# Prologue of a fused attention + MoE kernel: S by the second queue, k features from PSUM on three engines, a shorter token scale, smaller weight loads

## Chip, cores, metric

One core of a Trainium2 chip. The metric is the device time of one execution in microseconds (us), median of several runs. A kernel with one core has no second die to compare with, so a run's "state" is read from its time alone: **slow** is a run over 1.5% above the fastest run of the same kernel, all others are fast. In the profile PE is TensorE, PEld its weight loads, DVE VectorE, ACT ScalarE, POOL GpSimd, SP SyncE; a "q" behind a name is that engine's queue of DMA issues. L309 is line 309 of the kernel that the profile is of, so the same operation has another line in another kernel.

## The reference

```python
# q, k, v: (4 batches, 4 heads, 1088 tokens, 32); S1, S2: (8, 32); w_in (128, 2048), w_out (2048, 128)
def phi(x):                                  # 64 features: all products of two 8-wide projections
    a = einsum('rd,bhsd->bhsr', S1, x);  b = einsum('rd,bhsd->bhsr', S2, x)
    return einsum('bhsi,bhsj->bhsij', a, b).reshape(..., 64)
q_p, k_p = phi(q), phi(k)
kv = einsum('bhsf,bhsd->bhfd', k_p, v);  z = sum(k_p, axis=2)
x = einsum('bhsf,bhfd->bhsd', q_p, kv) / (einsum('bhsf,bhf->bhs', q_p, z) + 1e-6)
x = x.transpose(0, 2, 1, 3).reshape(4352, 128)
h = maximum(x @ w_in, 0);  out = (h * h) @ w_out        # all in fp32 at the boundary
```

## The kernel before

The loop over blocks of 384 tokens (FFN1, relu, square, FFN2, and the attention of later batches between them) is bound by TensorE and is all but untouched. What the change touches is the **prologue**: everything between the start and the first FFN2 matmul (tile `po`). Names to keep in mind: `s_T` is S1 and S2 transposed; `sk` and `sr` are spread copies of it; `kT` is k transposed; `kf` the projections of k, `kp` the 64 features of k; `kvp` collects the kv and z sums over nine tiles of 128 tokens; `rep` are the projections of q, each replicated over the rows that need it; `qp` the features of q; `nd` numerator and denominator; `xs` the scaled tokens that FFN1 takes. `keep_warm` issues fp16 matmuls of zeros with 512 columns, put there to bring TensorE to full clock.

```python
    WARM0, WARM = 9, 4
    ...
    nc.scalar.dma_start(s_nat[0:8, :], S1[:, :])          # ACT's queue
    load_qk(kn[0], k, 0, 0, 512)                          # SP's queue from here on
    nc.sync.dma_start(s_nat[8:16, :], S2[:, :])
    load_qk(kn[0], k, 0, 512, S)
    ...
    a_kT(0, 0)                                            # DVE transposes: kT first,
    nc.vector.transpose(s_T[:, :], s_nat[:, :])           # then S
    ...
    keep_warm(WARM0)
    a_kf(0, 0, psf, "pg");  a_fs(0, 0)                    # two tiles of k, ACT copies them out
    keep_warm(1, x0)
    a_kf(0, 1, psf, "pg");  a_fs(0, 1)
    ...                                                   # tiles 4 to 8 of k by another form
    replicated(2, ...)
    a_kp(0, 0);  a_kp(0, 1)                               # DVE: features of tiles 0 to 3
    ...                                                   # DVE: one transpose, features of tiles 4 to 8
    replicated(0, x0[:, 0:512])
    for t in range(4):  a_kv(0, t);  a_z(0, *st[0, "kp", t], False)
    ...
    for t in range(4, 9):  a_kv(0, t);  a_z(0, *st[0, "kp", t], t == 8)
    nc.scalar.copy(qb[:, :], rep[2][:, 0:384])
    products(0)                                           # DVE: features of q, first half
    replicated(1, x0[:, 512:1024])                        # into the tile that products(0) read
    a_kvz(0);  products(1);  a_set(2);  a_qT(0, 384, 768);  a_qT(0, 768, S)
    a_kvs(0);  a_nd(0, 0);  a_kvT(0);  a_kw(0)
    a_qc(0, 1, psf, "po")                                 # q projections of the next block
    keep_warm(WARM)
    a_x1(0, 0);  a_x2(0, 0)                               # token scale
    a_x3(...);  a_xp(...);  a_xT(...)                     # xs, transposed for FFN1
```

## Time and profile before

| | us |
|---|---|
| kernel before, runs beside the changed kernel | 193.72 median of 4 (193.23 to 194.33) |
| kernel before, all 50 runs of the study | 192.3 to 197.0 |
| span in its profile (the time less some 1.8 of launch) | 193.1 |

The profile that the prediction quotes was taken while TensorE ran at a quarter of its clock. In the prediction that quarter is my estimate; `b0_before` bears it out: the first warm-ups follow each other at 0.84 us in the quoted profile and at 0.43 in `b0_before`, and those at 14.56 us in `b0_before` at 0.21, a quarter of 0.84. So the first experiment, `b0_before`, runs the unchanged kernel once more and gives a profile at full clock; all readings of "before" below are from it. Its timeline, in columns start, duration, engine, line, operation, out<-in with the shapes, count, and in brackets how long the engine idled and what ended that:

```profile
1.00 3.75 PE L1055 MATMUL warm<-zero 128*128 128x512 f16 x9 [1.00 <-DVE s_nat L167]
...
4.90 0.63 PE L329 MATMUL kf<-sk,kT 128*128 128x64 f32 x4 [0.15 <-ACT sk L302]
...
7.24 1.53 PE L1083 MATMUL rep<-qT,sr 128*128 128x384 f32 x4
...
10.24 0.54 DVE L1088 TENSOR_TENSOR qp<-rep,qb 128x384 f32<-128x384 f32 x1
...
11.16 0.32 DVE L444 STREAM_TRANSPOSE kvt<-kvp 128x128 f32<-128x128 f32 x1 [0.38 <-PE kvp L405]
...
17.67 0.49 PE L931 MATMUL po<-g,w_o 128*128 128x128 f32 x2
```

The chain is: warm-ups up to `kf` at 4.90 with a gap of 0.15, the replications of q, the first product of q at 10.24 (early: `kvp` is still being summed), `kvt` at 11.16, the first FFN2 at **17.67**.

### The profile page before, as it was taken

What the parts mean: (1) busy time and instruction counts of PE and PEld (TensorE: products, weight loads), DVE (VectorE), ACT (ScalarE), POOL (GpSimd) and SP (SyncE); (2) the same over time, 40 slices, a digit from 0 to 9 for tenths busy, and PEclk for the clock granted to TensorE, in tenths of its full rate; (3) what the DMA queues carried; (4) which work ended last, traced back from release to release, by engine and by line L of the source; (5) the groups of instructions that cost most, each with busy time, mean ns of one, the idle gap of its engine ahead of it and who ended that gap; (6) DMA issues with size and microseconds to landing.
All of it is one profiled execution on the core that took longest, in us unless ns stands there. A gap on an engine that the chain in (4) does not pass through costs nothing.

```text
span 657.7 us, 4411 instructions
## 1 busy us (share of the span) xinstructions
PE 652.3 (99%) x1538; PEld 273.7 (42%) x1538; DVE 119.7 (18%) x284; ACT 138.6 (21%) x322; POOL 86.3 (13%) x168
## 2 busy tenths in 40 slices
PE   9999999999999999999999999999999999999997
PEld 3735333533343344333443335333343333333576
DVE  3141121121131111111040111220121111201120
ACT  2032222112222121221122121121221211211210
POOL 4011030020040101101130101101102110010000
DMA  7200200001100020010300010010010100000000
GB/s 226 74 1 0 74 1 12 1 18 40 41 18 0 0 60 0 1 30 0 80 13 5 0 25 1 0 30 1 0 30 1 25 0 0 12 0 0 13 0 10
DMA packets 29936, 13.92 MB, mean 21 GB/s; under 512 B 20186, under 2 KB 28506, under 8 KB 29914
## 3 DMA queue, kind: packets, MB, share of 16 engines
q1 hardware_dynamic: 29766, 13.58, 8.3%
q8 instruction: 12, 0.20, 0.1%
q14 instruction: 10, 0.08, 0.0%
q10 hardware_dynamic: 148, 0.07, 0.0%
HBM read 8.80 MB, written 2.23 MB: 17 GB/s over the span
## 4 chain that ended last, share of the span: by engine, by line
PE 99%; DVE 0%; ACT 0%; issue 0%
PE po L931 66%; PE pg L900 17%; PE kvp L391 2%; PE pt L948 2%; PE ndn L635 2%; PE warm L1055 2%; PE qk L562 2%; PE nd L776 1%; PE rep L1083 1%; PE qk L429 1%; PE ndn L702 1%; PE kvp L405 1%; PE qc L751 0%; PE kf L329 0%; PE ndn L548 0%; PE kvp L484 0%
## 5 line engine op out<-in xcount | busy, mean ns | idle before, releaser
L931 PE MATMUL po<-g,w_o 128*128 128x384 f32 (+3 forms) x386 | 489.2, 1408 | 0.0
L931 PEld LDWEIGHTS po<-g,w_o 128*128 128x128 f32 x386 | 167.1, 437 | 171.3 <-issue 115.3
L900 PE MATMUL pg<-xT,w_in 128*128 128x384 f16 (+2 forms) x193 | 161.7, 840 | 0.2 <-ACT xT L872 0.2
L910 ACT ACTIVATE gt<-pg 128x384 f32<-128x384 f32 (+2 forms) x136 | 64.1, 472 | 401.1 <-PE pg L900 397.5
L900 PEld LDWEIGHTS <-w_in 128*128 128x128 f16 x193 | 39.5, 205 | 126.8 <-issue 125.2
L894 ACT ACTIVATE g<-gt 128x384 f32<-128x384 f32 (+2 forms) x151 | 73.5, 497 | 50.2 <-DVE gt L912 50.1
L912 DVE TENSOR_SCALAR gt<-pg 128x384 f32<-128x384 f32 (+2 forms) x57 | 30.3, 532 | 276.1 <-PE pg L900 276.1
L921 POOL TENSOR_TENSOR g<-gt 128x384 f32<-128x384 f32 (+1 forms) x40 | 31.4, 786 | 310.0 <-ACT gt L910 310.0
L597 POOL TENSOR_TENSOR qp<-tq,bs 128x384 f32<-128x384 f32 (+1 forms) x18 | 14.2, 810 | 51.0 <-DVE bs L589 51.0
L359 POOL TENSOR_TENSOR kp<-fs 128x384 f32<-128x384 f32 x9 | 14.8, 1662 | 37.3 <-DVE fs L350 37.2
L391 PE MATMUL kvp<-kp,vn 128*32 128x64 f32 x288 | 19.1, 453 | 0.0
L391 PEld LDWEIGHTS kvp<-kp,vn 128*32 128x32 f32 x288 | 14.8, 189 | 8.9 <-issue 8.8
L948 PE MATMUL pt<-w_o,g 128*128 128x128 f32 x32 | 16.5, 672 | 0.0
L571 DVE STREAM_TRANSPOSE tq<-qk 128x384 f32<-128x384 f32 (+1 forms) x9 | 5.0, 561 | 62.7 <-PE qk L562 34.2
L736 POOL TENSOR_TENSOR bt<-s 128x384 f32<-128x384 f32 (+1 forms) x10 | 7.8, 783 | 63.3 <-DVE s L710 63.3
L948 PEld LDWEIGHTS pt<-w_o,g 128*128 128x128 f32 x32 | 13.7, 442 | 4.3 <-issue 2.7
L562 PE MATMUL qk<-qT,sw 64*32 64x192 f32 (+1 forms) x144 | 13.4, 831 | 0.0
L718 DVE TENSOR_SCALAR rs<-ndn 128x384 uint32<-128x384 uint32 (+1 forms) x9 | 4.8, 535 | 47.1 <-PE ndn L702 47.1
L1055 PE MATMUL warm<-zero 128*128 128x512 f16 x13 | 11.1, 1110 | 1.0 <-DVE s_nat L167 1.0
L977 DVE SCALAR_TENSOR_TENSOR sc<-po,bt 128x384 f32<-128x384 f32 (+1 forms) x9 | 4.8, 534 | 39.0 <-PE po L931 39.0
L417 PE MATMUL kvp<-fs 128*32 128x32 f32 x54 | 11.6, 363 | 0.0
L635 PE MATMUL ndn<-ft,kw 64*32 64x192 f32 (+1 forms) x144 | 11.4, 713 | 0.0
(147 smaller groups left out, 224.1 us busy)
## 6 DMA issues: line engine op xcount, KB each, us to landing
vn<-in_v_dram SPq DMA_DIRECT2D x32, 64.0 KB, 2.1
kn<-in_k_dram SPq DMA_DIRECT2D x3, 544.0 KB, 4.9
qn<-in_q_dram SPq DMA_DIRECT2D x3, 544.0 KB
ft<-u SPq DMA_DIRECT2D x24, 48.0 KB, 1.9
out_dram<-oT SPq DMA_DIRECT2D x24, 48.0 KB, 1.8
w_in<-in_moe_w_in_dram SPq DMA_DIRECT2D x2, 512.0 KB, 5.2
w_o<-in_moe_w_out_dram SPq DMA_DIRECT2D x2, 512.0 KB, 10.6
ft<-ft SPq DMA_DIRECT2D x12, 48.0 KB, 1.9
```

Source lines behind the costliest of these rows:

```text
L359: (nc.vector if g == 0 else nc.gpsimd).tensor_tensor(out=_ap(st[b, "kp2"], 0, 128, 128 * (NT * g + lo), [[64, 2 * (hi - lo)], [8, 8], [1, ...
L391: nc.tensor.matmul(st[b, "kvp"][32 * h : 32 * h + 32, 0:64], _ap(vn[b], 0, n, v0 + dv * h, [[1, 32]]), kp[0:n, at[h] : at[h] + 64], start= ...
L562: nc.tensor.matmul(qg[32 * o : 32 * o + 32, 512 * r : 512 * r + n], sw[b % 2][64 * r : 64 * r + 64, 32 * (o % 2) : 32 * (o % 2) + 32], qT[ ...
L635: nc.tensor.matmul(nd[32 * h : 32 * h + 32, 512 * g : 512 * g + n], st[b, "kw"][64 * g : 64 * g + 64, 32 * h : 32 * h + 32], st[b, ch, "ft ...
L894: nc.scalar.activation(dst, src, Square)
L900: nc.tensor.matmul(pg[:, c0:c1], w_in[:, 128 * c : 128 * c + 128], st[b, "xT"][:, 384 * ch + c0 : 384 * ch + c1],)
L910: nc.scalar.activation(gt[:, c0:c1], pg[:, c0:c1], Relu)
L912: nc.vector.tensor_scalar(out=gt[:, c0:c1], in0=pg[:, c0:c1], scalar1=0.0, scalar2=None, op0=amax)
L921: (nc.vector if on[1] == "DVE" else nc.gpsimd).tensor_tensor(out=g2[:, c0:c1], in0=gt[:, c0:c1], in1=gt[:, c0:c1], op=mult)
L931: nc.tensor.matmul(st["po", b, ch][:, c0:c1], w_o[:, 128 * c : 128 * c + 128], g2s[i][1][:, c0:c1], start=first, stop=(c == NFF - 1), skip ...
L948: nc.tensor.matmul(st["pt"][:, 0:128], g2s[i][1][:, 0:128], w_o[:, 128 * c : 128 * c + 128], start=(c == 0), stop=(c == NFF - 1),)
L1055: nc.tensor.matmul(t_[:, 0:512], zero[:, 0:128], _ap(zero, 0, 128, 0, [[0, 4], [1, 128]]))
```

## The change

Its intent, part by part: S1 and S2 both go out on ACT's queue, and `kT` moves behind `s_T`; the features of k are formed straight from PSUM, partly on DVE and partly on POOL, and POOL adds two pairs of tiles so that two of the nine z sums go; the epsilon of the denominator comes by two matmuls, so that the token scale has fewer small DVE operations; the weights come in smaller pieces in the order of need; and, moved along with these, `qc` and `a_set(2)` leave the prologue for the first steps of the loop. The diff also has smaller moves, such as the first load of v ahead of q's and other buffers for the loop's square; no run undoes these in the changed kernel, and `e16` below bounds what they can cost. Cut to the core:

```diff
-    WARM0, WARM = 9, 4
+    WARM0, WARM1, WARM = 8, 3, 5
 ...
     nc.scalar.dma_start(s_nat[0:8, :], S1[:, :])
+    nc.scalar.dma_start(s_nat[8:16, :], S2[:, :])
     load_qk(kn[0], k, 0, 0, 512)
-    nc.sync.dma_start(s_nat[8:16, :], S2[:, :])
     load_qk(kn[0], k, 0, 512, S)
 ...                                      # weights: 256 KB pieces, w_in first
+    load_w_in(0, 512)
     load_qk(qn[0], q, 0, 384, S)
-    load_w_in(0, nc.sync);  load_w_o(0);  load_w_in(1, nc.sync);  load_w_o(1)
+    load_w_in(512, 512);  load_w_o(0, 4);  load_w_o(4, 4);  load_w_in(1024, 1024);  load_w_o(8, 8)
 ...
-    a_kT(0, 0)
     nc.vector.transpose(s_T[:, :], s_nat[:, :])
+    a_kT(0, 0)
 ...
     keep_warm(WARM0)
-    a_kf(0, 0, psf, "pg");  a_fs(0, 0);  keep_warm(1, x0);  a_kf(0, 1, psf, "pg");  a_fs(0, 1)
+    kf0(kfa, ...) x2;  kpa = kp0(kfa, 0, 0, 2, nc.vector)
+    kf0(kfb, ...) x2;  nc.scalar.copy(fs, kfb);  kpb = kp0(fs, 0, 2, 2, nc.gpsimd)
+    keep_warm(WARM1, x0)
 ...
+    for t in range(4, 9): kf0(...)
+    kp0(kf4, ...) x2 and kp0(kf8, ...) on nc.vector
+    nc.gpsimd.tensor_tensor(out=kps, in0=kpa, in1=kpb, op=add)     # two z sums for four tiles
+    for t in range(4): a_kv(0, t)
     replicated(2, ...);  replicated(0, x0[:, 0:512])
 ...                                      # z of kps, kv and z of tiles 4 to 8
-    nc.scalar.copy(qb[:, :], rep[2][:, 0:384])
-    products(0)
-    replicated(1, x0[:, 512:1024])
-    a_kvz(0);  products(1);  a_set(2);  a_qT(0, 384, 768);  a_qT(0, 768, S)
-    a_nd(0, 0);  a_kvT(0);  a_kw(0);  a_qc(0, 1, psf, "po");  keep_warm(WARM)
-    a_x1(0, 0);  a_x2(0, 0);  a_x3(...)
+    replicated(1, x0[:, 512:1024], 0, 384)
+    products(0, 0, 384)                   # qb copied inside
+    a_kvz(0);  products(1, 0, 384);  a_qT(0, 384, 768)
+    nd_eps(nd0, 3);  nd_part(nd0, 0, 3)   # epsilon by two matmuls
+    x_part(nd0, 0, 3)                     # product before the maximum
+    a_kvT(0);  a_kw(0);  keep_warm(WARM)
 ...                                      # in the loop
+    a_set(2);  a_qT(0, 768, S)            # after the first FFN2
+        if i == 0: a_qc(0, 1, psf, "po");  a_qg(0, 2)
```

## The prediction

> **What bounds the kernel now.** I read the page's busy shares first, then the groups of instructions, then the timeline of the first 45 us, then the DMA issues. The change touches only the prologue (everything ahead of the first FFN matmul) and the first steps of the main loop, so the question is when that loop can start.
>
> ```profile
> span 657.7 us, 4411 instructions
> PE 652.3 (99%) x1538; PEld 273.7 (42%) x1538; DVE 119.7 (18%) x284; ACT 138.6 (21%) x322; POOL 86.3 (13%) x168
> ...
> L931 PE MATMUL po<-g,w_o 128*128 128x384 f32 (+3 forms) x386 | 489.2, 1408 | 0.0
> ...
> L1055 PE MATMUL warm<-zero 128*128 128x512 f16 x13 | 11.1, 1110 | 1.0 <-DVE s_nat L167 1.0
> ```
>
> The first thing to see is that this profile is not of the timed kernel: the span is 657.7 us against a median of 193.49. In the timeline the warm-up matmuls of 512 columns follow each other at 0.84 us, which is 0.61 columns per ns. [...] So TensorE ran at a quarter of its speed in the profile and I divide its durations by 4; DVE, ACT, POOL and DMA durations I take as they stand. "PE 99%" then says nothing about the prologue of a timed run.
>
> ```profile
> 1.00 7.37 PE L1055 MATMUL warm<-zero 128*128 128x512 f16 x9 [1.00 <-DVE s_nat L167]
> ...
> 3.45 0.71 DVE L293 STREAM_TRANSPOSE kT<-kn 128x512 f32<-128x512 f32 x1 [2.48 <-DMA kn<-in_k_dram]
> ...
> 4.09 0.16 DVE L300 STREAM_TRANSPOSE s_T<-s_nat 32x32 f32<-32x32 f32 x1
> 4.34 0.42 ACT L302 COPY sk<-s_T 32x16 f32<-32x16 f32 x2 [1.23 <-DVE s_T L300]
> ...
> 5.69 0.58 DVE L323 STREAM_TRANSPOSE qT<-qn 128x384 f32<-128x384 f32 x1
> ...
> 9.87 0.69 DVE L370 TENSOR_TENSOR kp<-fs 128x512 f32<-128x512 f32 x1 [3.60 <-ACT fs L343]
> ...
> 12.54 0.52 DVE L1099 STREAM_TRANSPOSE fs<-kf 128x320 f32<-128x320 f32 x1
> 13.09 1.56 DVE L1105 TENSOR_TENSOR kp<-fs 128x768 f32<-128x768 f32 x2
> ```
>
> Columns: start, duration, engine, line, operation. S is usable at 4.09 and its spread form sk at 4.76. The 3.60 us wait of DVE ahead of kp is an artefact of the slow TensorE: the warm-ups that end at 8.37 here would end near 4.8 at half speed (9 x 0.43), so kf is done by about 5.4 and DVE goes from qT (6.2) straight into the products. **At full clock DVE is the bound**: two products of 128x512 (0.69, overlapping to 0.62) end at 7.5, the transpose of 0.52 at 8.0, the two products of 1.56 at 9.6. TensorE meanwhile needs 2.6/4 = 0.65 for each of the two replications of q (6.3 to 7.65) and 0.84/4 = 0.21 for the kv and z sums of one tile; the last two tiles follow DVE, so kv ends near 10.2. Then come rep, kvz, products and nd (4.97/4 = 1.24): nd ends near 12.3.
>
> ```profile
> 32.36 0.17 DVE L790 TENSOR_SCALAR den<-nd 128x12 f32<-128x12 f32 x1 [3.48 <-PE nd L776]
> 32.45 0.55 DVE L795 TENSOR_REDUCE mx<-nd 128x12 f32<-128x384 f32 x1
> 32.91 0.22 DVE L800 RECIPROCAL rden<-den 128x12 f32<-128x12 f32 x1
> ...
> 33.97 0.69 DVE L836 TENSOR_TENSOR xs<-nd,sc 128x128 f16<-128x128 f32 x3
> ```
>
> This chain of small dependent operations takes 1.61 us to the first xs and 0.28 for that: 14.25. Transpose, xT (0.27), FFN1, relu (0.29) and square (0.31) bring the first FFN2 matmul to about 15.8.
>
> ```profile
> w_in<-in_moe_w_in_dram SPq DMA_DIRECT2D x2, 512.0 KB, 5.2
> w_o<-in_moe_w_out_dram SPq DMA_DIRECT2D x2, 512.0 KB, 10.6
> ```
>
> The first w_o load is issued at 8.17 and by its completion records lands at 16.2 (the second, issued 9.28, at 19.9). In the slow profile nothing waits for it; in a timed run the first FFN2 wants it at 15.8 and waits some 0.4. So the loop of the kernel before starts near **16.25 us**.
>
> [...] S1 from ACT and S2 from SP each took about 2.55 us from issue to landing. [...] Here the 128x384 square is 0.826 on POOL against 0.558 on DVE, 1.5 times.
>
> **The change part by part.**
> - S by ACT's queue. S1 goes at 0.95; ACT's issue took 0.59, so S2 goes at 1.54, and with 2.55 lands at 4.1 against 3.77 before. [...] I take s_T at 3.8, plus or minus 0.3. kT now stands behind s_T and the DVE copy of sk: s_T + 0.33 + 0.71 + wait, so kf starts at s_T + 1.1 = 4.9, against 4.8. No gain, unless S is early.
> - k features of batch 0. DVE sheds the 0.52 transpose and a 0.69 product (to POOL), but now idles about 0.7 us for kf and ACT's copy. Counting from kf's start K: first product K+0.7 to 1.4, kT K+2.05, qT K+2.7, products to K+4.4 = 9.3. DVE gains 0.3. But TensorE's tiles 4 to 8 (0.55) come only behind kT, kv of four tiles, and two replications: K+2.75, +0.45, +1.3.
> - GpSimd. Its product of 128x512: the 128x384 one has a median of 1.02, so about 1.35, from K+1.0; four sr copies of 0.24 follow, to K+3.35; then the sum of 128x512, 0.826 x 4/3 = 1.1, to K+4.45. z of kps waits for this about as long as TensorE is busy anyway. Four z groups become two, which saves 2 x 0.1 of TensorE. Then z 0.2 and five tiles 1.05: kv ends at K+5.95 = **10.85, 0.65 later** than before. TensorE's order and POOL have become the bound in DVE's place.
> - Token scale. Reciprocal 0.22, two products of 128x192 (0.33 each), reduction of 128x387 (about 0.5), mask 0.17, scale 0.25, with waits about 1.8 against 1.89: 0.1 saved. One transpose of qT (0.47) leaves DVE ahead of it, mostly hidden.
> - Weights. The first 256 KB of w_o should land well ahead of need, near 13 to 14, so the 0.4 wait goes.
> - qc (0.65 of TensorE) moves from the idle time ahead of xs into the first steps of the loop, next to qg; there some is hidden while ACT catches up. I charge 0.15.
>
> Sum against before, at the first FFN2: +0.65 -0.1 -0.4 +0.15 = +0.3 us. Two corrections go the other way. If the clock is still at half rate at 6.3, before's replications cost up to 1.3 more, while after's come a microsecond later; on average I take -0.3. And the warm-up count falls from 9 to 8, 0.43 us less, in a kernel tuned to the tenth; whoever set it must have seen kf ready about that much sooner, so S lands near 3.4: -0.4 to -0.5. Together **-0.5 us: 193.0**.
>
> **The rivals.**
> 1. S on one queue is late: the two ACT issues come one after the other, kf starts at 5.3, TensorE idles behind eight warm-ups and stays at half rate longer. For it: the 0.59 us issue. Against: the shortened warm-up. It would make 193.9 to 194.5.
> 2. GpSimd becomes the wait: TensorE waits for kpb, sr and kps in turn. For it: DVE products with both inputs in SBUF and POOL products slow each other (POOL's longest kp took 3.04 against 1.02). [...] 193.5 to 194.2.
> 3. The weights were the true bound: before waits for w_o longer than I think, and everything ahead of 16.2 is slack. Then the smaller loads alone give 0.5 to 1 and the rest moves the start: 191.8 to 192.7. For it: 10.6 us to landing. Against: a start at 15.8 leaves only 0.4 to win.
> 4. Every step is worth what the intent says (kf 0.4, DVE 0.3, z 0.2, weights 0.4, scale 0.3): 191.9.
>
> **Range and chances.** All of the prologue is 16 us and a 2% change is 3.9 us, a quarter of it; none of the rivals comes near. Range 191.7 to 194.2, from rivals 4 and 1. Faster by over 2%: 0.03; within: 0.95; slower: 0.02.
>
> **What would show it right or wrong.** In the changed profile (full clock or not): s_T's start tells whether S is early (3.4) or late (4.1); POOL's kp should last 1.35 and kps 1.1; the reciprocal to the first xs 1.5 to 1.6; the first w_o landing before 14.5. If TensorE again shows a quarter clock, its span will say nothing on the time. The prediction is wrong if a part moves the main loop itself, above all if qc and qg leave TensorE waiting for ACT in the first steps, or if the w_o wait was over a microsecond.

## The result

The changed kernel took **200.18 us** (200.10 to 201.57, 4 runs) against 193.72 (193.23 to 194.33, 4 runs): ratio 1.035, 95% interval 1.029 to 1.040. All ratios here are the mean time of one kernel's fast runs over the mean of the other's fast runs of the same rounds, so not quite the ratio of the medians quoted. The timeline of its profile (span 198.4 us):

```profile
0.93 0.59 ACTq L166 DMA_DIRECT2D s_nat<-in_S_dram  x1
...
1.03 3.60 PE L1114 MATMUL warm<-zero 128*128 128x512 f16 x8 [1.03 <-DVE zero L169]
...
1.54 0.29 ACTq L167 DMA_DIRECT2D s_nat<-in_S_dram  x1
...
4.52 0.20 DVE L309 STREAM_TRANSPOSE s_T<-s_nat 32x32 f32<-32x32 f32 x1 [3.55 <-DMA s_nat<-in_S_dram]
...
5.75 1.94 PE L1119 MATMUL kf<-sk,kT 128*128 128x64 f32 x8 [1.12 <-DVE kT L303]
...
8.76 2.23 PE L1119 MATMUL kf<-sk,kT 128*128 128x64 f32 x10
...
11.93 2.28 PE L1172 MATMUL rep<-qT,sr 128*128 128x384 f32 x4
...
15.63 0.91 PE L1172 MATMUL rep<-qT,sr 128*128 128x384 f32 x2
...
16.65 0.56 DVE L1182 TENSOR_TENSOR qp<-rep,qb 128x384 f32<-128x384 f32 x1 [3.82 <-PE rep L1172]
...
17.13 0.31 DVE L503 STREAM_TRANSPOSE kvt<-kvp 128x128 f32<-128x128 f32 x1
...
23.26 0.49 PE L990 MATMUL po<-g,w_o 128*128 128x128 f32 x2
```

**The loss is all in the prologue.** The first FFN2 comes at 23.26 instead of 17.67, 5.6 us later, and from there to the end of the span the two take 175.1 and 175.4 us. Three things are to be seen:

- The warm-ups end at 4.63, S comes at 4.52, `kT` stands behind it, and TensorE idles **1.12 us** ahead of `kf` (0.15 before).
- The same matmuls are slow. The trace's clock records, which the page rounds away at the start, give full clock from 4.35 us on in the kernel before and only from **13.42** in the changed one. `kf` x8 takes 1.94 here and 1.08 in a run below that had full clock, `kf` x10 2.23 against 1.33, `rep` x4 2.28 against 1.56.
- DVE waits 3.82 us for `rep`. It has what it needs when `rep` x4 ends at 14.2, but the product stands behind the third replication in the program, which writes into the same PSUM tile and comes after the last kv sums: 16.65. `kvt`, which could start when the kv sums end at 15.7, waits behind the product until 17.13.

The difference at `kvt` is 17.13 - 11.16 = 5.97 us. It can be laid out with the traces alone, taking from a run with mended clock and order (`e16_all_but_S`) that the same chain from `kf` to the end of kv takes 7.2 us at full clock (4.88 to 12.1): `kf` 0.85 later (5.75 - 4.90); 2.75 from half clock (9.95 from `kf` to 15.7, less 7.2); 1.43 from the order (15.7 to 17.13); 0.95 because the new arrangement is longer even at full clock (7.2 against 11.16 - 4.90 = 6.26). Whether the clock agrees with the stopwatch is for the experiments.

### The profile page after: what moved, and what is told of

Same layout as the page of the kernel before. It is cut to its first block, busy times and chain, and to the rows that moved or that the text cites. A ratio compares the mean times of both kernels' runs of the same rounds, so it can differ in the third digit from the quotient of the medians.

```text
span 198.4 us, 4388 instructions
## 1 busy us (share of the span) xinstructions
PE 188.0 (95%) x1522; PEld 113.3 (57%) x1522; DVE 116.6 (59%) x280; ACT 131.5 (66%) x327; POOL 89.0 (45%) x172
## 3 DMA queue, kind: packets, MB, share of 16 engines
HBM read 8.80 MB, written 2.23 MB: 56 GB/s over the span
## 4 chain that ended last, share of the span: by engine, by line
PE 72%; DVE 9%; SPq 4%; DMA 4%; issue 4%; POOL 3%; ACT 0%; ACTq 0%; DVEq 0%; POOLq 0%
PE po L990 44%; PE pg L959 12%; PE kvp L400 2%; PE kf L1119 2%; PE ndn L694 2%; PE pt L1007 2%; SPq L141 2%; DMA ft<-ft 2%; PE rep L1172 2%; POOL br L1022 1%; DMA s_nat<-in_S_dram 1%; PE qk L621 1%; POOL kp L368 1%; DMA ft<-u 1%; SPq L131 1%
## 5 line engine op out<-in xcount | busy, mean ns | idle before, releaser
L990 PE MATMUL po<-g,w_o 128*128 128x384 f32 (+3 forms) x386 | 143.9, 458 | 0.1
L990 PEld LDWEIGHTS po<-g,w_o 128*128 128x128 f32 x386 | 66.0, 190 | 33.1 <-issue 16.0
L959 PE MATMUL pg<-xT,w_in 128*128 128x384 f16 (+2 forms) x193 | 61.0, 317 | 0.5 <-ACT xT L931 0.3
L959 PEld LDWEIGHTS <-w_in 128*128 128x128 f16 x193 | 19.1, 99 | 22.1 <-issue 4.5
L656 POOL TENSOR_TENSOR qp<-tq,bs 128x384 f32<-128x384 f32 (+1 forms) x18 | 14.2, 812 | 17.3 <-DVE bs L648 17.3
L630 DVE STREAM_TRANSPOSE tq<-qk 128x384 f32<-128x384 f32 (+1 forms) x9 | 5.0, 561 | 12.1 <-PE qk L621 6.7
L400 PE MATMUL kvp<-kp,vn 128*32 128x64 f32 x288 | 6.9, 233 | 0.1
L400 PEld LDWEIGHTS kvp<-kp,vn 128*32 128x32 f32 x288 | 5.8, 116 | 2.0 <-PE pg L959 1.6
L368 DVE TENSOR_TENSOR kp<-fs 128x1152 f32<-128x1152 f32 x3 | 6.7, 2234 | 0.0
L332 DVE STREAM_TRANSPOSE qT<-qn 128x384 f32<-128x384 f32 (+1 forms) x12 | 6.4, 536 | 0.0
L694 PE MATMUL ndn<-ft,kw 64*32 64x192 f32 (+1 forms) x144 | 5.6, 325 | 0.5 <-DMA ft<-u 0.5
L1114 PE MATMUL warm<-zero 128*128 128x512 f16 x13 | 4.8, 534 | 1.0 <-DVE zero L169 1.0
```

Of the source, the lines that this page charges most:

```text
L368: (nc.vector if g == 0 else nc.gpsimd).tensor_tensor(out=_ap(st[b, "kp2"], 0, 128, 128 * (NT * g + lo), [[64, 2 * (hi - lo)], [8, 8], [1, ...
L400: nc.tensor.matmul(st[b, "kvp"][32 * h : 32 * h + 32, 0:64], _ap(vn[b], 0, n, v0 + dv * h, [[1, 32]]), kp[0:n, at[h] : at[h] + 64], start= ...
L656: nc.gpsimd.tensor_tensor(out=_ap(qp, 0, 128, 0, [[32, m], [8, 4], [1, 8]]), in0=_ap(st[b, "tq", ch], 0, 128, 4 * e, [[32, m], [1, 4], [0, ...
L694: nc.tensor.matmul(nd[32 * h : 32 * h + 32, 512 * g : 512 * g + n], st[b, "kw"][64 * g : 64 * g + 64, 32 * h : 32 * h + 32], st[b, ch, "ft ...
L959: nc.tensor.matmul(pg[:, c0:c1], w_in[:, 128 * c : 128 * c + 128], st[b, "xT"][:, 384 * ch + c0 : 384 * ch + c1],)
L990: nc.tensor.matmul(st["po", b, ch][:, c0:c1], w_o[:, 128 * c : 128 * c + 128], g2s[i][:, c0:c1], start=first, stop=(c == NFF - 1), skip_gr ...
```

## The experiments

My theory on reading the traces: gap, clock and order make the loss. The rivals: the arrangement of the k features by itself, the token scale, the weights. Later, when a rest remained, `qc` in the loop and the order of `kT` came in. All 18 runs gave the right result. Shown are the median, the ratio to the kernel before, and the first FFN2 in the profile.

| run | what | median us | ratio (95%) | first FFN2 |
|---|---|---|---|---|
| `b0_before` | before, unchanged | 194.86 | 1.008 (1.000 to 1.016) | 17.67 |
| changed kernel | | 200.18 | 1.035 (1.029 to 1.040) | 23.26 |
| `e1_warm11` | changed, WARM0 8 to 11 | 197.49 | 1.022 (1.013 to 1.031) | 20.48 |
| `e2_order` | changed, order undone | 199.57 | 1.031 (1.022 to 1.039) | 23.43 |
| `e3_S` | changed, S and kT undone, WARM0 9 | 198.48 | 1.014 (1.002 to 1.026) | 23.01 |
| `e4_warm11_8` | e1, and WARM 5 to 8 | 197.61 | 1.018 (1.012 to 1.024) | 20.94 |
| `e5_warm_order` | e4, order undone | 196.52 | 1.014 (1.010 to 1.017) | 19.77 |
| `e6_warm_order_S` | e5, S and kT undone, WARM0 9 | 195.49 | 1.008 (1.002 to 1.013) | 18.85 |
| `e7_before_warm6` | before, WARM0 9 to 6 | 195.56 | 1.009 (1.005 to 1.013) | 19.44 |
| `e8_before_S` | before, S2 on ACT, WARM0 10 | 193.35 | 0.993 (0.989 to 0.997) | 16.82 |
| `e9_before_scale` | before, new token scale | 194.84 | 0.999 (0.994 to 1.003) | 17.86 |
| `e10_before_weights` | before, new weight loads | 194.36 | 0.997 (0.994 to 1.001) | 17.42 |
| `e11_features` | before, new k features, mended order | 194.29 | 0.997 (0.994 to 1.001) | 18.47 |
| `e12_before_qc` | before, qc and qg in the loop, WARM 4 to 7 | 196.38 | 1.004 (0.997 to 1.011) | 17.09 |
| `e13_qc_back` | e5, qc, qg and setup back, WARM 5 | 195.77 | 1.007 (1.000 to 1.013) | 19.68 |
| `e14_S_warm11` | e8, WARM0 11 | 193.88 | 0.999 (0.993 to 1.005) | 18.92 |
| `e15_before_warm10` | before, WARM0 10 | 193.86 | 0.999 (0.993 to 1.004) | 16.87 |
| `e16_all_but_S` | e13, S and kT undone, WARM0 9 | 194.42 | 1.005 (1.000 to 1.009) | 18.43 |
| `e17_kT_first` | e13, kT ahead of s_T, WARM0 10 | 195.37 | 1.010 (1.006 to 1.014) | 19.54 |

**A caution first**: `b0_before` is the kernel before against itself, and came out at 1.008 with an interval that just leaves out 1. Single differences under about 1% are therefore not shown by these runs; what carries weight is the ladder as a whole and the traces. Also, since a slow run of this one-core program is known by its time alone, the fast means leave out the longest runs, whatever made them long: one of four in `e4`, two of five in `e3`, but also three of the seven runs of the kernel before in the session of `e4` to `e7`. By the medians of all runs of that session `e4` is 1.3% above the kernel before, `e5` 0.8%, `e6` 0.2% and `e7` 0.3%, so these ratios rather overstate the loss.

### The null run

> The kernel before, unchanged, to have a profile of it in the fast state. Clock theory (the change breaks the warm-up, so TensorE stays at half rate until 13.4 us after the change): here the clock must become full early, between 4.5 and 8 us, the replications of q must take about 0.65 us each pair, and the first FFN2 matmul must start near 16.3 us. Rival (the main loop changed, not the prologue): the first FFN2 matmul starts at 20 us or later here too, and the rest of the loop is several us shorter than the 175.1 us of the changed kernel. Time: the same as before within 0.3%.

194.86 against 194.24 in the same session: the noise of the method, and a profile at full clock. The first FFN2 came at 17.67, not near 16.3, but well ahead of the rival's 20; the prologue is what changed.

### e1: three more warm-ups

```diff
-    WARM0, WARM1, WARM = 8, 3, 5
+    WARM0, WARM1, WARM = 11, 3, 5
```

> The changed kernel with 11 warm-up matmuls in place of 8, nothing else, so that TensorE has no idle gap from 4.63 to 5.75 us. Clock theory: full rate between 5 and 8 us instead of at 13.4, and the half-rate work from 5.75 to 13.4 us (kf, kv, one replication: about 5 us of TensorE time, half of which goes) shrinks, so 2 to 3 us faster than the changed kernel: 197.2 to 198.2. Rival (late S and the DVE and GpSimd hand-overs set the pace, the clock does not): less than 0.5 us.

Measured 197.49, 1.022 against 1.035: the largest single step. It adds work and nothing else, so the kernel can only gain through the clock. The same rows of its timeline:

```profile
5.86 1.08 PE L1119 MATMUL kf<-sk,kT 128*128 128x64 f32 x8 [0.79 <-DVE kT L303]
...
8.14 1.33 PE L1119 MATMUL kf<-sk,kT 128*128 128x64 f32 x10 [0.55 <-DVE kT L303]
...
9.98 1.56 PE L1172 MATMUL rep<-qT,sr 128*128 128x384 f32 x4
```

`kf` starts no earlier (5.86 against 5.75), yet every matmul behind it has the short duration; `rep` starts at 9.98 instead of 11.93. The clock record says full from 4.09.

This profile alone does not show that the added warm-ups did it. At 4.09 the eighth warm-up was still running, so up to there TensorE had done the same as in the changed kernel. That the count matters is seen over the profiles: `kf` x10 took 2.23 us in both that have eight warm-ups (the changed kernel and `e2`), and 1.33 in all five of the changed kernel with ten or eleven (`e1`, `e4`, `e5`, `e13`, `e17`); with nine it took 2.23 in `e3` and 1.33 in `e6`, `e11` and `e16`. By the clock records full clock came at 13.42 and 16.06 in the two with eight, and at 6.16 in `e17`, with ten. When it comes differs from run to run: 4.09 in `e1`, 6.95 in `e4`, both with eleven. So a part of the 1.035, from four runs that all took 200.1 us or more, may be chance; `e2`, with the same eight warm-ups, also had runs of 198.35 and 198.97.

But the clock record of `e1` also says half from 21.16 to 24.57, and the page's row of granted clock shows it, in 40 slices of 4.9 us, as the 6 in the fifth:

```profile
PEclk9999699999999999999999999999999999999999
```

This is the second hole. The change took `qc` (0.65 us of TensorE) away from ahead of `xs` and put one more warm-up of 0.21 in its place; TensorE then idled 0.74 us ahead of the transposes of `xs`, and the clock fell for 3.41 us (`qc`, at 22.58, took 1.49 us; it took 0.81 at 24.72 in the changed kernel). In the changed kernel the same 0.74 us gap stands, and there the clock did not fall.

### e4: cover the second hole too

WARM0 = 11 and WARM = 8.

> The changed kernel with 11 warm-ups first and 8 in place of 5 ahead of the first transposes, nothing else. With 11 alone the clock became full at 4.1 us and fell back to half from 21.2 to 24.6 us, just behind a gap of 0.7 us in TensorE's work. Clock theory: early full rate, no fall back, first FFN2 matmul near 20.5 us as with 11 alone, and 1 to 1.7 us less than that run: 195.8 to 196.5. Rival (the fall back hits work that waits for ACT anyway): 197.2 to 197.5, as with 11 alone.

Measured 197.61, and not the 195.8 to 196.5 that I expected: the time is that of `e1`, as the rival had it, so covering the second hole is not shown to be worth anything. The clock was full from 6.95 on without a fall. With the clock covered the ratio is 1.018 instead of 1.035, and the two intervals do not meet.

### e2 and e5: the order

```diff
+    products(0, 0, 384)
     replicated(1, x0[:, 512:1024], 0, 384)
-    products(0, 0, 384)
```

> The changed kernel with the first product of q features put ahead of the third replication in program order, as the kernel before had it; the DVE then needs not wait for that replication. Order theory: the first product starts near 14.3 instead of 16.65 us, kvt at 15.8 instead of 17.13, and nd starts 1.2 to 1.5 us sooner: 198.7 to 199.0. Rival (nd waits for the second product and the third replication anyway, which are not sooner): 0.3 us or less.

> The same with the first product ahead of the third replication as well. Done alone, that order moved kvt no earlier, because in that run the clock became full 2.6 us later still (16.1 us). Order theory: with the clock held early, the first product starts near 11.6 and kvt near 13.0 in place of 14.46 us, and the first FFN2 matmul comes 1.2 us sooner: 194.6 to 195.3. Rival (order is worth nothing, the pace is set elsewhere): the same as the run with 11 and 8.

`e2`, on the uncovered clock, gave 1.031 and full clock only from 16.06 us: inconclusive by itself. With the clock covered, `e5` gave 196.52 us, more than the 194.6 to 195.3 that I expected, and 1.014 against 1.018 of `e4`, a difference that the stopwatch alone does not settle. The timelines do; first `e4`, then `e5`:

```profile
14.43 0.56 DVE L1182 TENSOR_TENSOR qp<-rep,qb 128x384 f32<-128x384 f32 x1 [2.46 <-PE rep L1172]
14.91 0.31 DVE L503 STREAM_TRANSPOSE kvt<-kvp 128x128 f32<-128x128 f32 x1
```

```profile
11.71 0.56 DVE L1182 TENSOR_TENSOR qp<-rep,qb 128x384 f32<-128x384 f32 x1
...
13.15 0.32 DVE L503 STREAM_TRANSPOSE kvt<-kvp 128x128 f32<-128x128 f32 x1 [0.89 <-PE kvp L414]
```

The product comes 2.7 us earlier, and what `kvt` waits for is now PE's last kv sum, as in the kernel before, and no longer DVE's own queue. `e5` ran with its timeline 0.39 ahead (the kv sums start at 9.46 against 9.85), so of the 1.76 us at `kvt` about 1.4 are from the order. At the first FFN2 (20.94 to 19.77) some 0.8 of these are left: in this profile `kvz` took 0.57 us against 0.29 in `e4`, and the two `xs` 0.93 against 0.63. Why they did is open.

### e3 and e6: S and kT as before

```diff
     nc.scalar.dma_start(s_nat[0:8, :], S1[:, :])
-    nc.scalar.dma_start(s_nat[8:16, :], S2[:, :])
     load_qk(kn[0], k, 0, 0, 512)
+    nc.sync.dma_start(s_nat[8:16, :], S2[:, :])
 ...
+    a_kT(0, 0)
     nc.vector.transpose(s_T[:, :], s_nat[:, :])
```

> The changed kernel with the S part undone: S2 on the first queue between the two k loads, the first k transpose ahead of the S transpose, and 9 warm-ups. Theory that S by the second queue costs: s_T starts near 4.1 instead of 4.52 us, kf near 4.85 instead of 5.75, the gap in TensorE's work closes, and with it the clock comes early too: 3 to 4 us faster than the changed kernel, 196.2 to 197.2. Rival (S is late by its own 0.4 us only and the clock does not matter): 0.9 us, 199.3.

> The same with S loaded as before too (S2 on the first queue, first k transpose ahead of the S transpose, 9 warm-ups up to kf at 5.0 us). Theory that S by the second queue costs its own 0.9 us beside the clock: where the clock comes early, the first FFN2 matmul starts at 18.4 us, 193.8 to 194.4; but with 9 warm-ups some runs have the late clock and are 2 to 3 us longer. Rival (S is not on the path once the clock is full): no faster than the run before this one.

`e3`'s five runs spread from 195.69 to 201.21, and its profiled run was a slow one (full clock from 13.78, half again from 24.02 to 27.43), so it says that nine warm-ups without the rest leave the clock to chance, not what S is worth. `e6`, with all three points mended, still lost 0.75% and its first FFN2 came at 18.85: the theory of gap, clock and order was not the whole.

### e7: fewer warm-ups in the kernel before

> The kernel before with 6 warm-ups in place of 9, so that TensorE idles from 3.6 to 4.9 us: the mirror of the change's gap, in the other kernel. Clock theory: [...] the clock becomes full between 8 and 14 us, and the time rises by 1.5 to 3 us over the kernel before: 195.5 to 197. Rival (the changed kernel is slow for its own structure, warm-ups matter little): within 0.3 us of the kernel before.

195.56, the low end of what I expected. The ratio of 1.009 is no larger than that of the null run, so the stopwatch does not settle it. The trace does: full clock only from 11.41 us, the first FFN2 1.8 us later than in `b0_before`, and `rep` x4 at 2.93 us, where it took 1.53:

```profile
4.89 1.08 PE L329 MATMUL kf<-sk,kT 128*128 128x64 f32 x4 [1.15 <-ACT sk L302]
...
7.79 2.93 PE L1083 MATMUL rep<-qT,sr 128*128 128x384 f32 x4
```

So the early clock of the kernel before, too, depends on its warm-ups.

### e9 and e10: token scale alone, weights alone

```diff
-    a_nd(0, 0)
+    nd_eps(nd0, 3);  nd_part(nd0, 0, 3)
 ...
-    a_x1(0, 0);  a_x2(0, 0);  a_x3(...)
+    x_part(nd0, 0, 3)
```

> The kernel before with only the new token scale (epsilon by two matmuls, product before the maximum). Theory (its seven operations take as long as the old eight because three of them work on 192 to 387 columns): from the end of nd to the first xs 1.75 to 1.85 against 1.6, first FFN2 17.6 to 18.0, time 0 to +0.4 us. Rival (the chain is shorter, as its intent says): -0.2 to -0.4 us.

The ratio is 0.999. The chain of DVE in its timeline:

```profile
13.52 0.23 DVE L469 RECIPROCAL rden<-nd 128x12 f32<-128x12 f32 x1 [0.40 <-PE nd L460]
13.79 0.62 DVE L475 TENSOR_TENSOR xf<-nd,rden 128x192 f32<-128x192 f32 x2
14.52 0.56 DVE L482 TENSOR_REDUCE mm<-xf 128x3 f32<-128x387 f32 x1
15.11 0.17 DVE L487 TENSOR_SCALAR rm<-mm 128x3 uint32<-128x3 uint32 x1
15.31 0.63 DVE L492 SCALAR_TENSOR_TENSOR xs<-xf,rm 128x128 f16<-128x128 f32 x2
```

13.52 to the start of `xs` at 15.31 is **1.79 us**; in `b0_before` the old chain ran from 13.74 to 15.36, 1.62. Fewer operations, and a longer chain, since the two products of 192 columns take 0.62 where the small operations took 0.17 each. Too little for the stopwatch.

```diff
-    load_w_in(0, nc.sync);  load_w_o(0);  load_w_in(1, nc.sync);  load_w_o(1)
+    load_w_in(512, 512);  load_w_o(0, 4);  load_w_o(4, 4);  load_w_in(1024, 1024);  load_w_o(8, 8)
```

> The kernel before with only the smaller and reordered weight loads. Theory (no first-block wait for w_o in the kernel before): first w_o data lands earlier by 1 us or more, yet first FFN2 17.5 to 17.9 and time within 0.2 us. Rival of the prediction (w_o waits 0.4): -0.3 to -0.5 us.

0.997 (0.994 to 1.001). The first pieces land sooner after their issue (median 6.8 us for 256 KB against 10.3 for 512), and the first FFN2 hardly moves: in `b0_before` it was released by ACT's square, not by `w_o`.

### e11: the k features alone

The kernel before with the new arrangement of features and z sums, and with `products(0)` where it was.

> The kernel before with only the new arrangement of k features and z sums of batch 0 (products on three engines, replications ahead of the last tiles), first product of q ahead of the third replication, nine warm-ups ahead of kf; S, token scale, weights and the place of qc as before. Theory (this arrangement is what is left of the loss once clock, order and S are mended): kvt 12.3 to 12.7 against 11.2, first FFN2 18.6 to 19.0, time +1.0 to +1.5 us. Rival (the rest is due to the token scale and the moved qc): kvt below 11.8, time +0.0 to +0.5 us.

I expected +1.0 to +1.5 us and was wrong: 0.997 (0.994 to 1.001). In its profile `kvt` does come late (12.12 against 11.16) and the first FFN2 at 18.47 against 17.67, but the rest of the span was 174.5 instead of 175.4 us, and the whole 193.0 against 193.1. Other profiles of kernels with the loop of the kernel before have rests of 174.0 (`e7`) to 175.1 (`e10`, `e15`), so a part of this is scatter of the loop. What the trace shows as 0.95 us in the prologue does not show on the stopwatch, and I leave that open.

### e8, e14, e15: S by the second queue in the kernel before

`e8` moves only S2's load (and has ten warm-ups), `e14` has eleven, `e15` has ten and nothing else.

> The kernel before with only S2 moved behind S1 on ACT's queue (kT still first on DVE) and ten warm-ups instead of nine, so that TensorE has no gap. Theory (the two issues in a row make S about 0.4 us later; that lateness alone is small and the loss in the changed kernel came from the gap and the clock): s_T at 4.4 to 4.6, kf at 5.3 to 5.6, full clock from 4 to 6 us, DVE's wait for the second part of k shorter by about 0.5 because that load is issued earlier; first FFN2 matmul 17.5 to 18.3, time +0.0 to +0.6 us. Rival (S late pushes the whole prologue by itself): first FFN2 above 18.7, +1 us or more.

> The kernel before with S2 on ACT's queue and eleven warm-ups (e8 had ten and was 0.7% faster). Theory (e8's gain is the second half of k, whose load is issued 0.6 us earlier; warm-ups only have to cover the wait): 0.99 to 0.996, as e8, or up to 0.3 us worse because the eleventh delays kf. Rival (e8's gain was luck with the clock): 0.998 to 1.003.

> The kernel before with ten warm-ups instead of nine and nothing else; it tells whether e8's gain came from its tenth warm-up. Theory (from S2's move): 0.999 to 1.003. Rival [...]: 0.991 to 0.996.

`e8` came out 0.7% faster. `e14`, the same with one more warm-up, did not (0.999), nor did `e15` (0.999), and the profiles of `e8` and `e15` have their first FFN2 at 16.82 and 16.87. No gain from the queue is shown, and **no loss** either, as long as `kT` stays first and the warm-ups reach to `kf` (at 5.23 in `e8`).

### e12 and e13: qc in the loop

> The kernel before with only qc, qg, the setup ahead of qg and the last transpose of q moved into the first steps of the loop, and seven warm-ups instead of four in the hole that qc leaves, so that the clock is kept. Theory (these operations were free ahead of xs, where TensorE idles, and cost their full length in the loop, where it is the bound): first FFN2 unchanged within 0.3 us, the first ten FFN2 matmuls stretched by 0.6 to 1.2 us, time +0.5 to +1.2 us. Rival (my prediction's 0.15 us, hidden behind ACT): time within 0.3 us.

> The changed kernel with eleven warm-ups ahead of kf, the first product of q ahead of the third replication, and qc, qg and the setup back ahead of xs with five warm-ups there; S, features, token scale and weights stay as changed. Theory (gap and clock, order, and qc are the whole loss): 193.7 to 195.0 us, ratio 0.995 to 1.004. Rival (something else of the change costs too, as parts that are harmless alone may collide): ratio 1.007 or more.

`e12` is inconclusive: its fast runs give 1.004 (0.997 to 1.011), but three of six runs were slow, and in the profiled one, a slow one, the clock had fallen from 18.37 to 21.78 us, and `qc` in it took 1.49 us. `e13` puts `qc`, `qg` and the setup back in the otherwise mended changed kernel: 1.007 against 1.014 of `e5`, above the 0.995 to 1.004 that I expected and at the rival's figure. What `qc` costs is plain in the two timelines. First `e5`, the first steps of the loop:

```profile
20.53 0.70 PE L990 MATMUL po<-g,w_o 128*128 128x256 f32 x2
...
21.23 0.81 PE L810 MATMUL qc<-qT,sq 128*128 128x384 f32 x2
...
22.02 0.51 PE L576 MATMUL qg<-qT,sqn 64*32 64x160 f32 x16
...
22.63 0.81 PE L990 MATMUL po<-g,w_o 128*128 128x384 f32 x2
```

and `e13`:

```profile
20.26 0.50 PE L576 MATMUL qg<-qT,sqn 64*32 64x160 f32 x16
...
20.70 0.70 PE L990 MATMUL po<-g,w_o 128*128 128x256 f32 x2
...
21.55 0.82 PE L990 MATMUL po<-g,w_o 128*128 128x384 f32 x2
```

From the first FFN2 matmul (19.77 and 19.68) to the third pair it is 2.86 us against 1.87: **1.0 us**. In `e13` `qg` runs while ACT and DVE prepare the second pair, and `qc` ran long before, in the hole ahead of `xs`; in `e5` both stand between two FFN2 matmuls. How much of it is left at the end of the span is less sure. From the first FFN2 on, these two take 174.65 and 174.30 us; the changed kernel, `e2`, `e4`, `e5` and `e6`, with `qc` in the loop, take 174.6 to 175.1, and `e13`, `e16` and `e17`, with `qc` ahead of it, 173.9 to 174.3.

### e16 and e17: what is left

> The changed kernel with the clock covered (nine warm-ups, S earlier), the first product of q ahead of the third replication, qc back ahead of xs, and S2 back on SP's queue with kT ahead of s_T. What is left of the change: k features and z sums on three engines, token scale, weights. Theory (the four undone points are the whole loss, and S with kT behind it is what held e13 back): kf at 4.8 to 5.1 against 6.1 in e13, ratio 0.995 to 1.003. Rival (the parts left collide with each other): ratio 1.006 or more, as e13.

> As e13, with S2 still on ACT's queue but kT transposed ahead of s_T, as in the kernel before, and ten warm-ups. Theory (not the queue but kT behind s_T is what made S's part dear): kf at 5.2 to 5.5 against 6.1 in e13, ratio 0.996 to 1.004. Rival (the queue itself): kf at 5.8 or later and ratio 1.005 or more.

`e13` still had `kf` at 6.11. `e16` puts S and `kT` back: `kf` at 4.88, ratio 1.005 (1.000 to 1.009). `e17` leaves S on ACT's queue and puts only `kT` first: `kf` at 5.62, ratio 1.010. Their first rows, `e16` and then `e17`:

```profile
4.11 0.16 DVE L310 STREAM_TRANSPOSE s_T<-s_nat 32x32 f32<-32x32 f32 x1
4.88 1.07 PE L1119 MATMUL kf<-sk,kT 128*128 128x64 f32 x8
```

```profile
4.81 0.20 DVE L310 STREAM_TRANSPOSE s_T<-s_nat 32x32 f32<-32x32 f32 x1 [0.60 <-DMA s_nat<-in_S_dram]
5.62 1.33 PE L1119 MATMUL kf<-sk,kT 128*128 128x64 f32 x8
```

With both loads on ACT's queue (in the changed kernel the first issue took 0.59 us and the second ended at 1.83) `s_T` came between 4.42 (`e8`) and 4.89 us (`e13`) in all nine profiles, with S on two queues between 4.10 and 4.23 in those of `b0_before`, `e3`, `e6`, `e7`, `e9` to `e12`, `e15` and `e16`, and there it is DVE's `kT` ahead of it that ends only then. `kT` behind `s_T` adds some 0.4 (`s_T` to `kf` is 1.22 in `e13` and 0.81 in `e17`). So the queue makes S at least 0.3 to 0.7 late and `kT` adds 0.4 to that; on the stopwatch `e17` is no better than `e13`, so I do not claim a time for `kT`. In that last session the ratio of `e16` is rather too high: four of the eleven runs of the kernel before were called slow and left out of the mean, and the medians of all runs are 194.42 and 194.09, 0.2% apart. Nothing that I ran is shown to be faster than the kernel before.

## Why the prediction was wrong

The loss of 3.5% is shown to come, for the most part, from four things together: 3.5% falls to 1.8 with the clock covered (`e1`, `e4`), to 1.4 with the order (`e5`), to 0.7 with `qc` back (`e13`), and to 0.5 with S as before (`e16`), whose interval reaches 1. The single steps below the first lean on the traces as much as on the times, and the first may hold some chance of when the clock became full.

By the steps of the prediction:

- **Rival 1, "S on one queue is late ... TensorE idles behind eight warm-ups and stays at half rate longer"**, was the right mechanism, though sized far too small at "193.9 to 194.5", and I gave it away for an inference. I set `s_T` at 3.8; it was 4.52. `kf` then came at 5.75, not 4.9; the step from `s_T` to `kf`, set at 1.1, was 1.23. S2's small load took some 2.85 us from issue (1.54) to landing (4.39), more than the 2.55 that I read for each of the two loads in the quoted profile (1.00 to 3.56 and 1.22 to 3.77).
- **"the warm-up count falls from 9 to 8 ... whoever set it must have seen kf ready about that much sooner"**: this gave -0.4 to -0.5 and has no number from a profile behind it. S was later and the count smaller, and the two together made the 1.12 us gap. This is the step that failed worst: it turned evidence for rival 1 into evidence against it.
- **"kv ends at K+5.95"** (its own terms add to K+5.75) measured K+9.95. About 2.75 of the difference is the half clock, for which I had no term on the changed kernel's side (I had even taken -0.3 for the kernel before); 1.25 was mis-sized at full clock (7.2 in `e16`). My figure for the kernel before was low by nearly as much (kv end 10.2 predicted, `kvt` at 11.16), so the difference between the two came out less wrong than either.
- **Missing altogether: the order.** I read that the third replication and the products come after kv and took them to stand as before. The product that stands behind a matmul into the other half of its PSUM tile waited for it here; that cost 1.4 us at `kvt`, some 0.8 at the first FFN2. It was visible in the diff, and in the order of each engine's instructions.
- **`qc`, "I charge 0.15"**, measured 1.0 in the trace by the third pair of FFN2 matmuls. Ahead of `xs` it ran while TensorE had nothing else to do; in the loop it stood between two FFN2 matmuls.
- **"so the 0.4 wait goes"**, the weights: there was no such wait. The estimate stood on a first FFN2 at 15.8; it is at 17.67.
- **Token scale, "0.1 saved"**: 0.17 lost. Up to the first `xs` the old chain was right (1.61, measured 1.62). The new one was mis-sized: the 1.8 included that `xs`, so 1.5 to 1.6 ahead of it, and 1.79 was measured.
- **Right, by and large**: POOL's product and sum at 1.35 + 1.1; measured 1.06 + 1.27, and neither bounds anything, so rival 2 was rightly set aside. Of "TensorE's order and POOL have become the bound" the first half was right. Rivals 3 and 4, which credited the weights and every intent, were wrong.

The range from 191.7 to 194.2 and the 2% for "slower" came from the argument that no rival comes near a quarter of the prologue. That holds for durations that add; it does not for a clock, which here made the matmuls behind it up to 1.8 times as long, all at once (`kf` x8 1.94 against 1.08).

## What to carry to other kernels

Count warm-ups not as filler but against the first matmul that they lead up to, and when a change moves that matmul later, ask whether they have to grow with it. Here the changed kernel moved that matmul from 4.90 to 5.75 us and took a warm-up away; full clock came at 13.42 instead of 4.35, and three more warm-ups were worth 1.3% of the time (1.035 to 1.022). For a later hole, from which the change takes work, that is not shown: the clock fell there in `e1` and not in `e4`, and the times are alike (197.49 and 197.61). Work that leaves a hole for a stretch in which the same engine is the bound can change from free to its full length, as `qc` did by the trace (1.0 us by the third pair of FFN2 matmuls). And when a diff moves a producer and its neighbour in one PSUM tile past a consumer, compare the program order on each engine before any durations: here DVE waited 3.82 us.

## What the traces leave open

- How much work it takes to bring the clock up. In the changed kernel TensorE was busy for all of the 7.67 us from 5.75 to 13.42, and the clock became full only at the end of that; in `e1` it became full at 4.09, 3.06 us after the first warm-up had begun.
- What makes it fall. In `e1` it fell behind a gap of 0.74 us ahead of the transposes of `xs`, in the changed kernel it did not behind a gap of the same length. Where it fell and rose again in the loop's first steps it was half for 3.41 us in `e1`, `e3` and `e12` and for 3.42 in `e14`.
- Why TensorE stood, just ahead of or between the transposes of `xs`, without any semaphore to wait for in three of the profiles: 0.34 us in `b0_before`, 0.98 in `e9`, 2.02 in `e14`, where the clock then fell from 19.14 to 22.56 us. The last one reads

```profile
17.41 0.33 PE L863 MATMUL xp<-iden,xs 128*128 128x128 f16 x3 [2.02 <-issue]
```
